# The gate in steps of four row groups, one wait for the row scatters of a half, a shorter warm-up and a new issue order

## The chip, the cores and the metric

The kernel runs on one core of a Trainium2 chip. The core has five engines that run their own instruction streams: TensorE (matmuls, PE in the profile, with its weight loads as PEld), VectorE (DVE), ScalarE (ACT), GpSimd (POOL) and SyncE (SP, which only issues transfers here). The metric is the time of one execution in microseconds on the device; the median over runs is compared.

## The reference, cut to what matters

A spectral layer is followed by a mixture of experts with two levels of routing.

```
X = rfft(x, axis=1)                                  # x: 8 x 1856 x 256
Y = soft_threshold(X @ (w_r + i w_i) + b, 0.01)      # real and imaginary part by themselves
x = irfft(Y).reshape(14848, 256)
...
g = argmax(x @ w_group); g_w = softmax at g           # 4 groups
e = argmax(x @ w_expert[g]); e_w = softmax at e       # 4 experts in the group
out[t] = g_w * e_w * (relu(x[t] @ w1[g, e]) @ w2[g, e])   # 256 -> 1024 -> 256
```

## The kernel before, in words

The 8 sequences are taken as 4 pairs. The first part of the program (up to about 476 us) works on the pairs one after the other, and overlaps the stages of one with those of its neighbours; the second part works through the experts.

Stages of a pair: the first transform's matmuls and VectorE's transposes of their results (`first_a`, L362, and `turn_a`, L403; for the last chunk of the first pair two half chunks, L411 and L414), 15 steps of the second transform and the weight matmuls (L697, L761) with splits into high and low parts on ScalarE and VectorE, then the inverse (`b_mm`, L809, `p_mm`, L828 and L831, with ScalarE's copies into the row tile in `p_out`, L839 and L841). The rows of a pair are in two halves of 16 row groups each. For eight units u of a pair, four to a half, TensorE turns the rows (`p_turn`, L850), ScalarE copies them to `yt` (L854), the gate's matmuls (`g_mm`, L871) form the logits of group and expert, and VectorE transposes these to `L` (`g_turn`, L881). Per half, `route_g` makes one-hot choices and slot numbers in 32 steps, mostly small VectorE instructions, and `scatter` (L305) writes the rows to a list for each expert in memory by GpSimd's indirect DMAs, 16 to a half, 128 in all. `FLY` says how many scatters are on their way at a time: two for the first three pairs, four for the last.

Eight early jobs of 256 rows (expert lists of the first 512 slots, 4 experts) are computed while the last pairs are routed: fetch of the rows by SyncE (`e_fetch`, L501 and L506; the first jobs wait for 64 scatters, the later ones for 96), transpose and split (L510, L936, L940), up matmuls (`up_mm`, L951), relu and split (L957, L961), down matmuls (`down_mm`, L972 and L973), scaling (L979, L984) and the store by GpSimd (`store`, L607). The second part, planned in `JOBS`, does the rest with the up matmuls in L549 and the down matmuls in L621 and L622.

In the first part the order of work is written out by hand: `ORDER` is a string with one letter for each step, and each letter calls the next step of its kind. On TensorE, ScalarE, VectorE and SyncE the instructions are issued in the order of the string. Letters used in this text: c and d the first transform and its transpose, o the end of a spectral step, v and w the inverse's last matmuls and copies, x and y the turn and its copy, G and H the gate's matmuls and their transpose, R a step of the routing, S one scatter, l a load on SyncE's queue, F an early job's fetch, W and V the split of an expert's weights, U and D the up and down matmuls of an early job (a quarter of each), K a store.

Ahead of all this, matmuls on constants warm TensorE up: 14 of 256 columns (L423) and 4 more (L427) ahead of the first data matmul, and 8 (L446) behind the second chunk.

Of the kernel before, what the change touches and what calls it, by code (L numbers as in the profile page):

```python
# [10 lines left out]
F32 = mybir.dt.float32  # L11
# [63 lines left out]


ORDER = """
efegjfhjihtugegiiktuekqpmqogpftmhmouccjkfeioqmhgotpjuimkmeqooftjphegudmiZmokcgqfhtoiujdpfktemqomhoupjmogimekfq
ocpghtjiukfdmqoehtmopgejiufmkmhqoetZgoupjgmkmidftqccioohudjpkmfmqehpcdgitmoofejmuhtoogkequgpjidmlkfitomcZqhopj
udmflkeoqpthmoujgimmfkqtoeZZhoujpemmfZkoogjqriphtfuesmsgokihrmoqjtpZfugsmskiZqmoehgrtoujpseimgskfrqihsmtosuepm  # L80
ofcdcdjkvvgiwhwoqtepmmcojZucdkfxqpmothuegoyxdjfimokqlyhvgcGwtdmocpjmilftukmHqhoeugpojximfketqygZhmpedocmfuojvg
himZwtdokeqpojugmkfxqyihmopmcdfvtuoGHjwRRvoRkqRepRhmwZiotjegRZRulikRRfxqmmtRhyoojpRugfegmRkZixqmptRZiRhyfomRoh
jvmuwGRokeRoqHgpjRxtmRmuRyRifRRtooleghkqirupjRsmRksofZtqhmoursjepmRkRmvqgRRfooihewjtRgsupxmmRReoikyfSoqtghrjsu
iGpfkSsHrRRqhetRmmpRgSoRSSsfmsohSuiSRjtcvkRmeRuqRpedgcowmcofmRljhRioSekdqdRtxypgRuoRvgfvjSwiSkxRwRyqitpchmvGRl
omufmdocRmjRhRtRkeHqdpwgReRucmiofgoScjhmRkdoRSiqoxSRyStRSpxjRuRfmmkqooReypRdcjmgthvduGRHfmioRRRtvRRwkegqwRpohi
mReSSRxuRfjkohRRmRegSiyRlSSqRtxRRuSpojSRkSvymfvRmwgShRoGRqSRwStpoHuxRjfmhiykemRqtSoRgSoRRRjSixypufRmhRmeoSokRq
tGHRSjRSrpRumkRseSsgimSqSfrRohptuSogeisRSjfRgsmRhkimqrSotRoRpsjeSufshmSmokgotjrWqpRumiWsfRRkqmResShopovRgRmRlt
oujmwSivkRoReqRRjfhptRSguxRkRfSRwimehmRqRSptWooRxuRRjmRykSqmRfygReitopSgohvvVfhiuSSSwGSjVxWSeSVkwRWmxygtVymHqp
WSGmviuHvoofjmkRRheoqRRRRwRRoRwRjtRSRpmRVugSRovfmvRRiekSwRVtgRRqSRwxhpojuSiRfekxRRhmmytRRoSlqogSRuRSRSpjyRmRfR
SixWWxGSkmhoHqytSouySSVRegjiVpmkmqoofGhtpujHRRRkmRqRRpSoRRRRSRmoSRmSmooFRTRRRXrRYSURRssFRSUSABrARRBRSsUsSRRRRR  # L90
RRrUsAARsSBBDIrWWDIlssVDvWVEwvTXDVSSwxYxWVSSUSyvyJvGWSHARBwESwxxSyUySWGHRRvRRvRRSRUwRwRxAWVRSRSBWSVVxAURyyRvRR
RlwSRvJGSSwxRxRRRRVHASRSFByKFBRyRRRDRDTXRYRRGHUAERSBURADSUBFUTASDXSRRJRDBAWYVEBKJSSWUWRRRUIDKTRlAWIESBRRDVRSRA
BRURURDSVVAXJRRDSRABERYRWBWDKFSWlJFRUUVKRVETDAWAWIRJWBUWVVBFVVAUSVBXRRYDRREASURSRBSDKUJlSRDRAWVWWKDABWUSBESVUV
DKASWTJDXBSASYBTSISSVUVDSESUAASJSSKSSRBKUEISDBUJADXYDABUBDKUIEAJBEKAUBDUAJBKADBEDDJDDKEJKEJK
"""

_OFF = {}
# [88 lines left out]
def spectral_moe(ctx: ExitStack, tc: tile.TileContext, x, wri, bri, wgate, w1, w2, cst, out):  # L186
    nc = tc.nc
# [108 lines left out]
        nc.vector.tensor_tensor(out=base, in0=base, in1=incf.rearrange("p (e r) -> p e r", e=NE)[:, :, n - 1], op=ALU.add)  # L296
        yield

    pend, sent, sent_of = [], [], []
    landed = mybir.DependencyInfo(mybir.DependencyClass.Sync, mybir.DependencyReason.DATA)  # L300

    def scatter(n):
        for _ in range(n):
            pr, sl_, row = pend.pop(0)
            ins = nc.gpsimd.indirect_dma_start(out=xs_d, out_offset=bass.IndirectOffsetOnAxis(ap=sl_, axis=0), in_=row,  # L305
                                               in_offset=None, bounds_check=ROWS - 1, oob_is_err=False)
            if len(sent) >= FLY[pr]:
# [29 lines left out]
    rt = inv.enter_context(tc.tile_pool(name="rt", bufs=1))  # L337
    ci = inv.enter_context(tc.tile_pool(name="ci", bufs=1))
    wi = inv.enter_context(tc.tile_pool(name="wi", bufs=2))
# [79 lines left out]
            pass  # L419

    warm = pg.tile([128, 512], F32, name="pg")
    for _ in range(14):
        nc.tensor.matmul(warm[:, 0:256], lhsT=ones, rhs=smask[16], start=True, stop=True)  # L423
    for _ in range(2):
        y = pw.tile([128, 512], F32, name="pw")
# [14 lines left out]
    for i in range(7):  # L440
        o = bank()
        first_a(0, i, o)
        turn_a(0, i, o)
        if i == 1:
            for _ in range(8):
                nc.tensor.matmul(warm[:, 0:256], lhsT=ones, rhs=smask[16], start=True, stop=True)  # L446
    for h in range(2):
        last_half(h)
# [199 lines left out]
    wts, raws, low, units, psum = {}, {}, {}, {}, {}  # L648
# [18 lines left out]
    pairs, later, u8, k15 = range(NP), range(1, NP), range(8), range(K1)  # L667
# [165 lines left out]
    yts = {}  # L833

    @steps_of(pairs, u8)
    def p_out(pr, u):
        o = psum.pop(("p", pr, u)).rearrange("p (h s b d x) -> p b x s h d", h=2, s=4, b=2, x=2)
        y = four(pr, u).rearrange("p b x (s h d) -> p b x s h d", s=4, h=2)
        nc.scalar.copy(out=y[:, 0], in_=o[:, 0])  # L839
        for h in range(2):  # L840
            nc.scalar.copy(out=y[:, 1, :, :, 1 - h], in_=o[:, 1, :, :, h])  # L841

    @steps_of(pairs, u8)
    def p_turn(pr, u):
# [5 lines left out]
                nc.tensor.transpose(o[:, c:c + 128], rows[:, i // 2, i % 2, ch * 128:ch * 128 + 128], ident)  # L850

    def p_copies(pr, u, copy):
        yts[pr, u] = wi.tile([128, 2, 4, 128], F32, name="yt", bufs=2)
        copy(out=yts[pr, u], in_=psum.pop(("t", pr, u)).rearrange("p (c r t) -> p c r t", c=2, r=4))  # L854

    copies = iter([(pr, u) for pr in pairs for u in u8])
# [3 lines left out]
            p_copies(*next(copies), copy)  # L860
            yield

    @steps_of(pairs, range(0, 8, 2))
    def g_mm(pr, u):
        psum["g", pr, u] = pg.tile([128, 512], F32, name="pg")
        o = psum["g", pr, u][:, 0:256].rearrange("p (h v z) -> p v h z", h=2, v=2)
        for v in range(2):
            yt = yts.pop((pr, u + v)).rearrange("p c (h x) t -> p c h x t", h=2)
            for ch in range(2):
                for q in range(4):  # L870
                    nc.tensor.matmul(o[32 * q:32 * q + 32, v], lhsT=wg[:, ch], rhs=yt[:, ch, :, :, 32 * q:32 * q + 32],  # L871
                                     start=ch == 0, stop=ch == 1)
# [574 lines left out]
```

## Time and profile before

| | us |
|---|---|
| three runs | 1066.43, 1066.68, 1061.5 (median 1066.43) |
| the profiled execution | 1063.61 |
| its span from the first to the last instruction | 1061.8 |
| TensorE busy | 1015.5 (96%) |
| VectorE busy | 698.5 (66%) |
| ScalarE busy | 545.9 (51%) |
| GpSimd busy | 259.1 (24%) |

The rows further down come from the profiled execution. Matmuls are pipelined and their ends are modelled, so a TensorE that counts as busy is not always at its peak. An engine's idle time matters where it is the one that others wait for. "issue" and "remote" as the reason of a wait say that the profile shows nothing that ended it.

### The profile page before, as it was taken

What the parts mean: (1) busy time and instruction counts of PE and PEld (TensorE: products, weight loads), DVE (VectorE), ACT (ScalarE), POOL (GpSimd) and SP (SyncE); (2) the same over time, 40 slices, a digit from 0 to 9 for tenths busy, and PEclk for the clock granted to TensorE, in tenths of its full rate; (3) what the DMA queues carried; (4) which work ended last, traced back from release to release, by engine and by line L of the source; (5) the groups of instructions that cost most, each with busy time, mean ns of one, the idle gap of its engine ahead of it and who ended that gap; (6) DMA issues with size and microseconds to landing.
All of it is one profiled execution on the core that took longest, in us unless ns stands there. A gap on an engine that the chain in (4) does not pass through costs nothing.

```text
span 1061.8 us, 20038 instructions
## 1 busy us (share of the span) xinstructions
PE 1015.5 (96%) x7094; PEld 863.6 (81%) x7094; DVE 698.5 (66%) x1744; ACT 545.9 (51%) x1428; POOL 259.1 (24%) x267
## 2 busy tenths in 40 slices
PE   8999999899898987899999999999999999999996
PEld 5886887587776676788889989999889899889995
DVE  5888789688789555546667656466465566566551
ACT  3765675575783642334554445355354455454541
POOL 2000003236354545441112111211111212112121
PEclk9999999999999998999999999999999999999998
DMA  9435552332134354446434241432341420732100
GB/s 375 183 142 199 202 221 88 112 119 77 42 109 116 108 135 131 154 121 195 135 113 111 69 133 33 140 112 55 119 141 38 141 81 26 193 115 58 37 26 26
DMA packets 110932, 125.63 MB, mean 118 GB/s; under 512 B 86869, under 2 KB 87643, under 8 KB 105965
## 3 DMA queue, kind: packets, MB, share of 16 engines
q1 hardware_dynamic: 91549, 74.28, 23.8%
q0 software_dynamic: 12448, 30.68, 7.8%
q10 hardware_dynamic: 6832, 19.36, 4.7%
q8 instruction: 57, 0.93, 0.4%
q14 instruction: 46, 0.38, 0.1%
HBM read 74.32 MB, written 51.65 MB: 119 GB/s over the span
## 4 chain that ended last, share of the span: by engine, by line
PE 85%; issue 4%; DVE 4%; POOL 1%; DMA 1%; ACT 1%; another core or an unknown queue 1%; SPq 0%; POOLq 0%; DVEq 0%; ACTq 0%
PE ph L549 25%; PE py L621 16%; PE pw L761 12%; PE py L622 8%; PE pg L697 5%; PE ph L951 4%; PE bank L809 3%; PE bank L362 2%; PE bank L850 2%; PE pg L972 2%; PE bank L828 2%; PE pg L871 1%; PE pg L973 1%; PE py L641 1%
## 5 line engine op out<-in xcount | busy, mean ns | idle before, releaser
L621 PE MATMUL py<-big,hh 128*128 128x512 f32 (+2 forms) x792 | 276.4, 393 | 0.3 <-DVE yo L629 0.3
L549 PE MATMUL ph<-xth,big 128*128 128x384 f32 (+17 forms) x1024 | 274.1, 345 | 1.1 <-DVE hl L557 0.7
L607 POOL DMA_INDIRECT out_dram<-yo,si x119 | 122.9, 1033 | 495.0 <-DVE si L327 239.2
L557 DVE SCALAR_TENSOR_TENSOR hl<-ph,hh 128x256 fp32r<-128x256 f32 x472 | 157.5, 372 | 97.7 <-ACT hh L553 70.8
L622 PE MATMUL py<-big,hl 128*128 128x256 f32 (+2 forms) x792 | 220.8, 279 | 0.0
L553 ACT ACTIVATE hh<-ph 128x256 fp32r<-128x256 f32 x472 | 140.0, 345 | 112.9 <-PE ph L549 109.9
L305 POOL DMA_INDIRECT xs_d<-v,sloti x128 | 127.4, 995 | 289.4 <-DVE xs L736 157.4
L549 PEld LDWEIGHTS ph<-xth,big 128*128 128x128 f32 x1024 | 185.6, 188 | 13.1 <-ACT xth L535 1.2
L549 PE MATMUL ph<-xtl,big 128*128 128x384 f32 (+17 forms) x512 | 176.5, 345 | 0.9 <-DVE xtl L536 0.6
L621 PEld LDWEIGHTS py<-big,hh 128*128 128x128 f32 (+2 forms) x792 | 147.1, 186 | 34.9 <-issue 0.8
L622 PEld LDWEIGHTS py<-big,hl 128*128 128x128 f32 (+2 forms) x792 | 147.5, 186 | 0.4
L629 DVE SCALAR_TENSOR_TENSOR yo<-py,si,yo 128x256 f32<-128x256 f32 (+3 forms) x99 | 47.8, 482 | 108.4 <-ACT yo L628 104.1
L628 ACT ACTIVATE yo<-py,si 128x256 f32<-128x256 f32 (+3 forms) x99 | 46.8, 473 | 130.7 <-PE py L622 109.1
L549 PEld LDWEIGHTS ph<-xtl,big 128*128 128x128 f32 x512 | 96.5, 188 | 6.1 <-DVE xtl L536 1.1
L761 PE MATMUL pw<-wh,xh 128*128 128x256 f32 x360 | 81.1, 307 | 6.1 <-issue 2.7
L783 ACT ACTIVATE th<-pw,sg 128x256 f32<-128x256 f32 x120 | 60.5, 525 | 38.3 <-PE pw L761 26.8
L761 PEld LDWEIGHTS pw<-wh,xh 128*128 128x128 f32 x360 | 54.4, 189 | 28.4 <-issue 7.0
L761 PE MATMUL pw<-wl,xh 128*128 128x256 f32 x360 | 71.6, 280 | 0.2 <-issue 0.2
L761 PE MATMUL pw<-wh,xl 128*128 128x256 f32 x360 | 71.5, 280 | 0.0
L697 PE MATMUL pg<-CF,big 128*128 128x128 f32 x480 | 64.5, 277 | 4.1 <-DVE xs L736 3.1
L697 PEld LDWEIGHTS pg<-CF,big 128*128 128x128 f32 x480 | 58.4, 191 | 11.6 <-issue 3.9
L951 PE MATMUL ph<-xth,big 128*128 128x256 f32 x256 | 54.0, 298 | 6.7 <-ACT xth L936 3.2
(197 smaller groups left out, 1563.5 us busy)
## 6 DMA issues: line engine op xcount, KB each, us to landing
xt<-in_w_dram SPq DMA_DIRECT2D x22, 1024.0 KB
xs_d<-zero ACTq DMA_DIRECT2D x16, 1170.0 KB
whole<-in_w_dram SPq DMA_DIRECT2D x16, 1024.0 KB
xt<-in_x_dram SPq DMA_DIRECT2D x8, 1024.0 KB
xg<-xs_d SPq DMA_DIRECT2D x48, 96.0 KB
v<-in_x_dram SPq DMA_DIRECT2D x4, 1024.0 KB
big<-in_x_dram SPq DMA_DIRECT2D x7, 512.0 KB
xg<-xs_d SPq DMA_DIRECT2D x24, 128.0 KB
```

Source lines behind the costliest of these rows:

```text
L305: ins = nc.gpsimd.indirect_dma_start(out=xs_d, out_offset=bass.IndirectOffsetOnAxis(ap=sl_, axis=0), in_=row, in_offset=None, bounds_check ...
L549: nc.tensor.matmul(o[:, :w], lhsT=a_[:, ch, fs], rhs=b_[:, ch, 0:w], start=k == 0, stop=k == 5)
L553: nc.scalar.activation(out=hh[:, f, :m], in_=ov, func=AF.Relu)
L557: nc.vector.scalar_tensor_tensor(out=hl[:, f, :m], in0=ov, scalar=0.0, in1=hh[:, f, :m].bitcast(F32), op0=ALU.max, op1=ALU.subtract)
L607: ins = nc.gpsimd.indirect_dma_start(out=out, out_offset=bass.IndirectOffsetOnAxis(ap=ids.si[0:m, t:t + 1], axis=0), in_=ysb, in_offset=No ...
L621: nc.tensor.matmul(o, lhsT=hh[:, f, ts], rhs=w2b[:, :, f, :], start=f == 0, stop=f == 7, skip_group_check=True)
L622: nc.tensor.matmul(o[:, 0:D], lhsT=hl[:, f, ts], rhs=w2h[:, f, :], start=False, stop=f == 7, skip_group_check=True)
L629: nc.vector.scalar_tensor_tensor(out=ysb, in0=o[:, 0:D], scalar=gate_w, in1=ysb, op0=ALU.mult, op1=ALU.add)
L697: nc.tensor.matmul(f_view(pr, k)[:, ch, :, bt], lhsT=zys[pr][:, k, bt, ch * 128:(ch + 1) * 128], rhs=T_v[:, k, :], start=True, stop=True)
L761: nc.tensor.matmul(y[:, half * D:(half + 1) * D], lhsT=a_[:, ch, t], rhs=w_[:, t, ch], start=False, stop=True, skip_group_check=True)
L783: nc.scalar.activation(out=units["t", pr, k][:, ri], in_=psum["m", pr, k][:, ri * D:(ri + 1) * D], func=AF.Relu, bias=nlam, scale=sg_col(0 ...
L951: nc.tensor.matmul(o[:, i * 256:(i + 1) * 256], lhsT=a_[:, ch, fs], rhs=b_[:, ch, :], start=k == 0, stop=k == 5)
```

## The change

The gate takes four units in one step where it took two: 64 matmul instructions of the profile fill a whole bank of 512 columns, and one transpose of 128x512 follows. There are 8 such steps instead of 16; `yt` has four buffers instead of two and `L` one instead of two. `p_out` notes the last of its copies for each unit, and the first scatter of each half gets a dependency on the last copy of that half, so that the later scatters of the half need no wait for the copies. The warm-up has 8 and 3 matmuls where it had 14 and 8. The order string is new from the first line to the last; it has eight G and eight H less and is otherwise made of the same letters.

```diff
-efegjfhjihtugegiiktuekqpmqogpftmhmouccjkfeioqmhgotpjuimkmeqooftjphegudmiZmokcgqfhtoiujdpfktemqomhoupjmogimekfq
...
+ejfegifhteguijtkhuqkpegmmqgfopoijhtmmucfoikeqotgjhpukeqfimhgpcZtomdfmouoicjkZethuZqmojdgpikmfqoepthmojeufgdkgi
...
-    pend, sent, sent_of = [], [], []
+    pend, sent, sent_of, written = [], [], [], {}
...
+            if len(sent) % 16 == 0:
+                tc.add_manual_dep(ins.ins, written[pr, len(sent) % 32 // 4 + 3], landed, reason="later rows of the half need no wait of their own")
...
-    for _ in range(14):
+    for _ in range(8):
         nc.tensor.matmul(warm[:, 0:256], lhsT=ones, rhs=smask[16], start=True, stop=True)
...
-            for _ in range(8):
+            for _ in range(3):
                 nc.tensor.matmul(warm[:, 0:256], lhsT=ones, rhs=smask[16], start=True, stop=True)
...
         for h in range(2):
-            nc.scalar.copy(out=y[:, 1, :, :, 1 - h], in_=o[:, 1, :, :, h])
+            ins = nc.scalar.copy(out=y[:, 1, :, :, 1 - h], in_=o[:, 1, :, :, h])
+        written[pr, u] = ins.ins.name
...
-        yts[pr, u] = wi.tile([128, 2, 4, 128], F32, name="yt", bufs=2)
+        yts[pr, u] = wi.tile([128, 2, 4, 128], F32, name="yt", bufs=4)
...
-    @steps_of(pairs, range(0, 8, 2))
+    @steps_of(pairs, range(0, 8, 4))
     def g_mm(pr, u):
         psum["g", pr, u] = pg.tile([128, 512], F32, name="pg")
-        o = psum["g", pr, u][:, 0:256].rearrange("p (h v z) -> p v h z", h=2, v=2)
-        for v in range(2):
+        o = psum["g", pr, u].rearrange("p (h v z) -> p v h z", h=2, v=4)
+        for v in range(4):
...
-    @steps_of(pairs, range(0, 8, 2))
+    @steps_of(pairs, range(0, 8, 4))
     def g_turn(pr, u):
-        if u % 4 == 0:
-            logits[pr, u // 4] = rt.tile([128, 16, 32], F32, name="L", bufs=2)
-        L = logits[pr, u // 4].rearrange("p (h i) m -> p h i m", h=2)[:, :, 2 * (u % 4):2 * (u % 4) + 4]
-        nc.vector.transpose(out=L, in_=psum.pop(("g", pr, u))[:, 0:256].rearrange("p (h i m) -> p h i m", h=2, i=4))
+        logits[pr, u // 4] = rt.tile([128, 16, 32], F32, name="L")
+        L = logits[pr, u // 4].rearrange("p (h i) m -> p h i m", h=2)
+        nc.vector.transpose(out=L, in_=psum.pop(("g", pr, u)).rearrange("p (h i m) -> p h i m", h=2, i=8))
```

## Rows read from the trace of the kernel before

**Rows 1.** Busy time by stretch; columns: stretch, length, engines, granted clock, DMA, GB/s.

```profile
0.00:20.00 20.00, 15.99 (x114) 7.36 (x114) 11.42 (x16) 5.27 (x9) 7.18 (x10) 1.00 0.93 360
20.00:155.00 135.00, 134.50 (x1197) 109.45 (x1198) 109.96 (x232) 89.89 (x214) 0.00 (x0) 1.00 0.54 207
155.00:330.00 175.00, 161.06 (x1532) 125.07 (x1534) 142.95 (x350) 111.43 (x261) 70.09 (x70) 0.99 0.28 95
330.00:386.00 56.00, 51.58 (x469) 36.00 (x461) 36.67 (x82) 27.90 (x55) 27.52 (x28) 0.97 0.30 93
386.00:476.00 90.00, 78.93 (x493) 70.43 (x494) 48.75 (x114) 31.66 (x62) 45.05 (x47) 0.92 0.47 142
476.00:1062.00 586.00, 573.43 (x3298) 515.29 (x3296) 348.73 (x954) 279.74 (x829) 109.30 (x113) 0.99 0.33 96
```

**Rows 2.** The same view for four short stretches; engines are PE, PEld, DVE, ACT, POOL.

```profile
265.00:276.00 11.00, 8.26 (x62) 6.05 (x58) 6.57 (x16) 4.21 (x10) 6.35 (x7) 0.84 0.22 77
374.00:382.00 8.00, 5.55 (x52) 4.46 (x42) 4.01 (x11) 3.29 (x7) 3.23 (x4) 0.79 0.38 98
402.00:423.00 21.00, 15.27 (x65) 11.78 (x64) 9.07 (x24) 5.79 (x13) 11.33 (x12) 0.76 0.48 143
441.00:450.00 9.00, 5.41 (x25) 4.67 (x24) 3.25 (x7) 1.11 (x2) 6.21 (x7) 0.81 0.28 97
```

**Rows 3.** VectorE's timeline: start, length, instruction, idle ahead of it and its reason.

```profile
379.54 0.45 DVE L881 STREAM_TRANSPOSE L<-pg 128x256 f32<-128x256 f32 x1 [3.92 <-remote]
```

**Rows 4.** The chain of waits: start, length, what.

```profile
374.61 2.27 DMA xs_d<-v,sloti
...
380.26 3.78 DMA xg<-xs_d
...
468.54 1.43 PE ph L951 x12
```

**Rows 5.** TensorE's timeline at an early job and at the first main job.

```profile
386.30 0.39 PE L951 MATMUL ph<-xtl,big 128*128 128x256 f32 x1 [0.34 <-DVE xtl L940]
...
476.80 0.34 PE L549 MATMUL ph<-xth,big 128*128 128x392 f32 x1
```

**Rows 6.** The timeline of TensorE and VectorE in the first 18 us.

```profile
1.52 3.15 PE L423 MATMUL pg<-smask,ones 128*128 128x256 bf16 x14 [1.52 <-DVE smask L213]
...
5.45 2.13 PE L362 MATMUL bank<-big,cA 64*64 64x512 f32 x16
...
7.51 1.05 PE L446 MATMUL pg<-smask,ones 128*128 128x256 bf16 x8
...
9.64 6.23 DVE L403 STREAM_TRANSPOSE big<-bank 128x1024 f32<-128x1024 f32 x5 [0.46 <-PE bank L362]
```

**Rows 7.** Groups of instructions before 476 us: busy, mean ns, idle ahead and reasons.

```profile
L871 PE MATMUL pg<-yt,wg 128*32 128x128 f32 x512 | 17.7, 276 | 0.9 <-DVE xl L730 0.6 <-issue 0.3
...
L881 DVE STREAM_TRANSPOSE L<-pg 128x256 f32<-128x256 f32 x16 | 7.1, 441 | 18.4 <-PE bank L828 8.2 <-PE pg L871 5.5 <-remote 3.9
...
L414 DVE STREAM_TRANSPOSE big<-bank 128x512 f32<-128x512 f32 x2 | 1.4, 695 | 0.2 <-PE bank L411 0.2
```

**Rows 8.** GpSimd: the scatters' timeline, and the extra wait instructions of L305 (last).

```profile
174.17 0.97 POOL L305 DMA_INDIRECT xs_d<-v,sloti  x1 [0.93 <-DMA xs_d<-v,sloti]
...
184.00 0.97 POOL L305 DMA_INDIRECT xs_d<-v,sloti  x1 [0.43 <-issue]
...
387.81 0.97 POOL L305 DMA_INDIRECT xs_d<-v,sloti  x1 [9.67 <-DVE base L296]
...
434.01 0.97 POOL L305 DMA_INDIRECT xs_d<-v,sloti  x1 [0.31 <-issue]
...
460.75 0.97 POOL L305 DMA_INDIRECT xs_d<-v,sloti  x1 [0.30 <-issue]
...
L305 POOLq EVENT_SEMAPHORE  x46: 17/17/24911, 145.5 to 456.2; - x46
```

**Rows 9.** SyncE's timeline at the first main job.

```profile
463.52 0.38 SPq L501 DMA_DIRECT2D xi<-xs_d  x1
```

More of the change, by code (lines that the diff above doesn't have):

```diff
@@ L77 @@
 ORDER = """
-efegjfhjihtugegiiktuekqpmqogpftmhmouccjkfeioqmhgotpjuimkmeqooftjphegudmiZmokcgqfhtoiujdpfktemqomhoupjmogimekfq
[L79 to L92, printed above, removed]
@@ L93 @@
-BRURURDSVVAXJRRDSRABERYRWBWDKFSWlJFRUUVKRVETDAWAWIRJWBUWVVBFVVAUSVBXRRYDRREASURSRBSDKUJlSRDRAWVWWKDABWUSBESVUV
-DKASWTJDXBSASYBTSISSVUVDSESUAASJSSKSSRBKUEISDBUJADXYDABUBDKUIEAJBEKAUBDUAJBKADBEDDJDDKEJKEJK
+ejfegifhteguijtkhuqkpegmmqgfopoijhtmmucfoikeqotgjhpukeqfimhgpcZtomdfmouoicjkZethuZqmojdgpikmfqoepthmojeufgdkgi
+hccmmqotojidpumkeoqfhpmtojufgkmdqomepciohtjmumogfokjqeitgphudmkfeZqpilghmtucifoohtcjdmmkqooepugjkidmqmftooejph
+ukgimfomqehptogjuimkemqoofjthupmmgoefkorhqjiptgufmsskieZZomqrogtjpheusZksmimfoogqrhZjituspkmqfepmsgothilorfhus
@@ new lines @@
+emsjgtekmucvqdiopwgfmcvZoZidjmowothkvvwujqpwfkmemgqopmtmohjxfyuoehxykqxitpoZjuekxqfgihypymlcdtummomfgojGvHoioc
+ktjRheqpudgmkRliqReofhgimotjupewRkZqfhtvmgRcRRmiRdpwcoocRumejkmdfoxoytqdRpmjhucovkdgRmfeoRRqihtujRwpmxRkRRgRoi
+eZqymofpgRthjixmemRyuooRkRfgqtrhpuRslsZjRRmkRZfrReoihqtspgmsouvfjewgkihmtxqyiRopmmuRrosfjGhkmotsqeHRgRuZRrpojs
+mRRklemSqgRsSRoRopfhvjimtRcuedmokwgqcvRiSpSidfcwSRRhomtjuRRvRkRoRfewmSqhgRpeoStijmukfxdRqgmthpSiSSRyfeumomgoij
+vhoRwSRRckqegdtpoxjxlumoyfRkxRqRphRilyRytmumSRfcRcotdGSdScSmvRhoRRRlojkuqSHRewjpgmidRmfRtRSkSeqpmRSRhSRSfovRgS
@@ new lines @@
+oomRcRhjeuowitkSjxygqpuRfdmmkeSqRRpvRovSiRRoStRgRmifjhuhRmkRqwSooteRpwugxjmSRfRkxyqoSmxRRitRpyheoRyujRRmRRgefR
+mhSSkqSSriRpGotgsiomfsutHorhessjRugikemrgRqopsSSSRjskmfmtqRohorpujRsseRmRkfWmRivvRSWSSwqtRpoSRRRWhogjRRxRuRmRR
+SSkfSihewRRSRoyvvRRmotgRqpuRjwikRRSRfRmRmeqwxgotVhpSioxyeSVmujWkxVyqfphoVtyGvSfhRHmSomlWRogjmSRvRuiRweRRRSkxRt
+WoSqRpjVwSugSRkRSRRqfimRSSoRSxtpSyyhemeSRfomSRRuvoRRggvhjkwRiRSRSmxwqRtRpiySWouRRjRxfRymRRhemogkSSoRGtuqHSjRil
+kRqSpRRmRfopRtmeRmhoumofgSSojithkuRSqRjkSRRpSRRqmpRmRRVmRRoSRmRRooSorRFTXRYSsFURsRrRRRSABsUIUAsSARrBRWDVSRSUss
@@ L95 @@
+ArVBBWWTSXDSsDSsSSWvvSYWwwDvRvSwVSEVVUAxwyESUxSlBASVJWUBJVxyWxyUSvySvGwAWVwvHSVASvRDBWwwSRRxIBFRVRFyTKlxRRDXRD
+lREYRyJDxRRRUURRFxRARBRRABRREUyRUTyARJRKKRXRGYRRAWBRBDRWTKUURRAABDUHVWIRSRIRBWUREXRDIRSJRRFDARSRVWVYRRVBABRlWE
+RRSVJRRSSSWDURSSKSVWVAWFVSUIWDDSASFSSlRDEKSVBJWUVBEJURWATRRRDRBARXBWVYRRRDRUWKURRSAASVSVSBIDUSVSBSWWEKJUDRSTVD
+SSAABXVBEYUSTDAEBJKSSUDAUBSSUDASXKEIBJDYABUJAUABKDDKBUAEUJDKADBEBDJDDKEJKEJK
 """
```

## The prediction

> **What bounds the kernel now.** I read the busy time of every engine by stretch first [rows 1]. From 476 us on TensorE is busy 573.4 of 586 us, at a clock of 0.99. Nothing in the diff is executed there, and 12.6 us of idle in 586 leave little to move. The same holds from 20 to 155 us: 134.5 of 135. TensorE is idle for 4.0 us before 20 us, 13.9 us from 155 to 330, 4.4 us from 330 to 386 and 11.1 us from 386 to 476: 33 us, and these are the places that another order can reach. VectorE is the runner-up from 20 to 330 us, with 253 of 310 us (82%), and drops to 54% after 386 us.
>
> Next I looked at where those idle stretches cost twice. Four windows [rows 2] hold a TensorE idle time and, right after it, a lower granted clock: 0.84, 0.79, 0.76 and 0.81 as means, which is some time at the half level (1.2 of 2.4 GHz). Each is priced as idle plus lost clock: 2.74 + 0.16 x 11 = 4.5 us; 2.45 + 0.21 x 8 = 4.1 us; 5.73 + 0.24 x 21 = 10.8 us; 3.59 + 0.19 x 9 = 5.3 us. Together 24.7 us of a 1061.8 us span. In all four several engines stand at once and the profile names mostly "issue" or "remote" as the cause, so I cannot say what ends them, only who stands where. In the second, VectorE stood 3.92 us at L881, the first of the two gate transposes of the last half, until 379.54 us [rows 3].
>
> Third, the chain of waits from 343 to 392 us [rows 4]: it runs through the row scatters on GpSimd's queue to the last scatter that the third early job needs (374.61), the fetch of its rows (380.26) and its first up matmuls. But TensorE itself waited only 0.34 us for that job [rows 5]; until then it had other steps to do. So the scatter queue is the longest chain there and still worth almost nothing on TensorE by itself.
>
> **The change part by part.**
>
> *Shorter warm-up.* Before the first data matmul 6 of 14 warm-up matmuls go, 3.15/14 = 0.225 us each, 1.35 us; behind the second chunk 5 of 8 go, 1.05/8 = 0.13 us each, 0.66 us [rows 6]. The first data matmul starts at 5.45 us, right behind the warm-up, so it is the warm-up that holds it and not its data. What counts is VectorE's transposes: five of them run without a gap from 9.64 us, and only the third had to wait, 0.46 us, behind the second warm-up block. Their data arrive meanwhile: 16 DMA engines are 0.93 busy in the first 20 us at 360 GB/s [rows 1], and the eight chunks of 524 KB and the weights' 524 KB need 4.7 MB / 360 GB/s = 13.1 us behind the first issue at 0.7, so the last half chunk cannot be much earlier than 14 us, where its matmul starts about 2 us later. Gain at most 1.35 + 0.46 = 1.8 us, at least nothing. I take 0.5, as the transfers and not the matmuls become what is late. On the other side, fewer warm-up matmuls may leave data matmuls at the half clock: the ratio is 0.225 to 0.13 for the same 256 columns, so the 2.13 us of the first two chunks would be 3.7 us, 1.6 us more, and with a third chunk some 2.4 us, of which 0.5 are regained: +1.9 us. That is the other bound.
>
> *The gate in steps of four row groups.* The 512 matmul instructions stay [rows 7]; a step is 64 instead of 32 (17.7/16 = 1.1 us, then 2.2 us). On VectorE 16 transposes of 128x256 (0.441 us each, 7.1 us) become 8 of 128x512; such a transpose from PSUM takes 0.695 us (L414), so 5.6 us: 1.5 us less. VectorE has 82% work before 330 us, so I count half of it, 0.7; bounds 0 and 1.5. In front of the 16 transposes VectorE stood idle for 18.4 us [rows 7], because it takes its instructions in order and the transpose comes before the gate's matmuls are done. Eight of those places vanish, and each of the others waits for 1.1 us more matmul and four copies instead of two. If all eight were exposed that is 8 x 1.1 = 8.8 us lost; if the waits halve, 9.2 us of VectorE idle is gained, most of it after 330 us, where VectorE has room. At nothing, then, but for the one place below. Four yt buffers for a step of four and two for a step of two give ScalarE the same wait (the copy after a full step waits for that step's matmuls); nothing, and one step of 2.2 us on ScalarE where the order leaves no cover. One L buffer instead of two: its reader and its writer are both VectorE instructions in order, nothing.
>
> *Scatters.* Each row scatter is 0.97 us on GpSimd. Where it needs a second wait, an extra wait instruction stands ahead of it (46 of them [rows 8]) and the idle before it is typically 0.93 us, without one 0.43 us. In the six halves with two scatters in flight, rows 2, 4, 6 and 14 have such a wait: 6 x 4 x 0.5 = 12 us of queue time go. The added dependency on the half's last copy sits on the first row, which waits anyway for its slot numbers, made from logits that come from those same copies: nothing. In the last two halves, with four in flight, the idle is 0.3 us with or without it. For TensorE the queue counted 0.34 us, so I take 0.3; bounds 0 and 4 us (the two halves ahead of the third early job).
>
> *The order.* Both strings hold the same letters but for eight G and eight H less. Counted by letters, ahead of the ninth U (the third early job's start) the new order has the same U, v, W and V, two D more and 18 R less: the last halves' routing moves behind it. Ahead of scatter 96 (first row of the seventh half) stand six U and four D more; ahead of scatter 112 one U and one D less. The loads l1 to l7 stand later in SyncE's queue, where nothing but loads stands at that time, and l13 to l15 earlier, l13 now ahead of the fetch of the fifth early job; the weight split that frees its buffer stands ahead of it in both strings, so the fetch is not held. No count shows less matmul work in front of any milestone, so the order can only win or lose idle time, up to 33 us plus the lost clock. The place where it plainly differs is the second stall: the VectorE instruction that stood there no longer exists, and the seventh and eighth halves' routing runs elsewhere. I take this one stall as gone, 4.1 us, and the others as staying. Bounds: none gone (0) and the two largest gone (10.8 + 5.3 = 16 us) on one side; the rival below on the other.
>
> **Sum.** The profiled execution took 1063.6 us (span 1061.8 and 1.8 around it), 0.3% under the median of 1066.43; the three runs shown lie between 1061.5 and 1066.7. 1063.6 - 0.5 - 0.7 - 0.3 - 4.1 = 1058.0 us.
>
> **A rule of the skill that speaks against the warm-up cut.** The Trainium skill, "TensorE: Matmul & The Clock Gate", section "Part 1: The HAM clock gate (the "warmup" mystery)", says that an array that has been idle begins at its lower clock and is raised only after sustained activity. The trace agrees so far: the first warm-up block runs at 0.225 us a matmul, the second at 0.13 [rows 6]. By that rule the cut would give the +1.9 us above in place of -0.5.
>
> **Rivals.**
>
> *Only the small terms arrive.* The stalls are not tied to the gate; they come back at other steps. For it: the first of the four lies in the spectral stage and the last two in early-job steps, none of which the gate touches, and nothing names their cause. Against it: VectorE's place in one of them is taken out. 1063.6 - 1.5 = 1062 us.
>
> *Two or more stalls go.* For it: the order is new from end to end. Against it: a new order meets its own hazards as well. 4.1 + 5.3 + 1.5: 1053 us.
>
> *The late halves end too late (slower).* The seventh half's scatters began at 387.81 us, the last half's at 434.01, the last one at 460.75; the first main job's rows are fetched at 463.52 [rows 8, 9] and its matmuls start at 476.80 [rows 5]. Six U and four D at 1.4 us each [rows 4] push the seventh half by 14 us to about 402; its 16 rows at 0.97 + 0.31 us and some five stores fill the queue to 429, so 5 us of cover are left, and the main job's rows have some 4 us more: for the third early job the way from the last scatter to the matmuls was 386.3 - 374.6 = 11.7 us [rows 4, 5], and 460.75 + 11.7 = 472.5. If the last scatter slips more than 9 us, TensorE waits. Slipping 15 us costs 6 us plus a half-clock stretch of 1.7 us: 1063.6 - 1.5 + 7.7 = 1070 us. For it: the whole of the routing of the last half stands behind more work. Against it: ahead of scatter 112 stand one U and one D less than before, and fewer stores stand between the last scatters.
>
> *The clock stays low at the start.* Everything else as forecast: 1058 + 2.4 = 1060 us.
>
> **How the numbers follow.** One stall gone 0.45 (own range 1054 to 1062), small terms only 0.20, two stalls gone 0.10, late halves 0.17, low clock 0.08. A difference under 0.5% (5.3 us, under 1061.1 or over 1071.8) is about what cannot be told from no change. Faster: 0.36 of the forecast's 0.45, the 0.10 and 0.02 of the low clock, 0.48. Slower: 0.12 of the late halves and 0.03 of the other cases, 0.15. The rest, 0.37, is no change. The range 1051 to 1067 leaves out the lower end of the two-stall case and most of the late halves, some 0.18.
>
> **What would show it.** Right: the first data matmul near 4.1 us at the full rate and the third transpose up to 0.5 us earlier; eight transposes at L881's place near 0.7 us with less idle than 18.4 us in sum; 20 to 24 extra waits fewer on GpSimd; no window like 374 to 382 us with a low clock; the first main matmul at about 471 instead of 476.8 us, and from there the same 585 us to the end. Wrong: the same number of half-clock stretches; a fetch for the first main job later than 463.5 us; or a main part that changes its own length, which I hold at nothing.

## The result, and the profile after

The kernel after takes 1077.66 us (median of four runs, 1073.92 to 1081.11) against 1064.59 of the kernel before (four runs, 1061.5 to 1066.68): a ratio of 1.0106, 95% interval 1.0068 to 1.0144. It is slower; the forecast was 1058.0 us, range 1051 to 1067. The profiled execution of after took 1081.11 us, with a span of 1079.2.

Busy time by stretch, kernel after, columns as in [rows 1] (length, PE, PEld, DVE, ACT, POOL, granted clock, DMA share, GB/s):

```profile
0.00:20.00 20.00, 14.39 (x103) 5.92 (x103) 11.43 (x16) 5.70 (x10) 7.15 (x10) 1.00 0.93 362
20.00:155.00 135.00, 134.29 (x1174) 109.50 (x1178) 109.70 (x231) 91.19 (x216) 0.00 (x0) 1.00 0.50 189
155.00:330.00 175.00, 157.94 (x1458) 123.04 (x1451) 130.80 (x312) 104.02 (x240) 65.96 (x67) 0.94 0.27 97
330.00:386.00 56.00, 50.10 (x399) 36.45 (x398) 36.99 (x77) 25.22 (x54) 28.11 (x29) 0.97 0.30 90
386.00:495.00 109.00, 92.70 (x662) 80.55 (x662) 59.63 (x148) 41.98 (x82) 49.96 (x51) 0.92 0.47 137
495.00:1080.00 585.00, 571.81 (x3294) 513.77 (x3292) 348.43 (x954) 279.50 (x829) 108.75 (x112) 0.99 0.33 96
```

The timelines of GpSimd, SyncE and TensorE around the end of the first part:

```profile
416.23 0.97 POOL L305 DMA_INDIRECT xs_d<-v,sloti  x1 [4.92 <-ACT hh L959]
...
476.72 0.97 POOL L305 DMA_INDIRECT xs_d<-v,sloti  x1 [0.30 <-issue]
...
479.48 0.38 SPq L503 DMA_DIRECT2D xi<-xs_d  x1
...
494.89 0.28 PE L975 MATMUL pg<-big,hl 128*128 128x256 f32 x1
495.01 0.34 PE L551 MATMUL ph<-xth,big 128*128 128x392 f32 x1
```

The first main matmul (L549 before, L551 after; most lines moved by two) starts at 495.01 us, not at 476.80 [rows 5]. From there to the end it is 584.2 us, before 585.0. So all of the loss, 18.2 us in the two traces, lies in the first part. Up to 155 us the two kernels run alike: 134.3 of 135 us, before 134.5. From 155 to 330 us TensorE idles for 17.1 us (before 13.9), and the granted clock is 0.94 (before 0.99) [rows 1].

Two counts of my own carry the rest; both are worked out from the records of the two traces. *Idle under the bursts*: a half's 16 scatters are a burst, from the start of the first to 3 us behind the start of the last. TensorE idles for 27.3 us under the eight bursts of the kernel before and 37.9 us under those of after, and for 2.1 and 1.3 us in all the rest from 165 to 490 us. *Half clock*: the clock is granted at its half level in 5 stretches of together 20.5 us before, in 9 of together 41.0 us after, the end of the program left out. The changes from 165 to 490 us are 10.6 - 0.8 = 9.8 us of idle under and outside the bursts, and 20.5/2 = 10.2 of lost clock: 20.0 us, somewhat over the 18.2, since part of the half-clock time is idle itself. The first 20 us hold 1.6 us more idle, but there 1.8 us of warm-up matmuls are gone. All four stall windows of [rows 2] lie in or just behind a burst as well. Bursts are frequent, though: in the kernel before they cover 232 of the 325 us from 165 to 490.

The scatters' waits, kernel after (the extra waits, then two reasons of idle time ahead of scatters, with their counts):

```profile
L305 POOLq EVENT_SEMAPHORE  x22: 17/17/15163, 154.2 to 472.7; - x22
...
  DMA xs_d<-v,sloti: 45.6, 51
  issue: 23.4, 69
```

24 of the 46 extra waits [rows 8] are gone. Of the 120 steps from one scatter of a half to the next, 87 are shorter than 1.5 us, before 77, and the bursts are 9 us shorter together.

### The profile page after: what moved, and what is told of

It reads as the page before. It is cut to its first block, busy times and chain, and to the rows that moved or that the text cites. A ratio compares the mean times of both kernels' runs of the same rounds, so it can differ in the third digit from the quotient of the medians.

```text
span 1079.2 us, 19960 instructions
## 1 busy us (share of the span) xinstructions
PE 1021.2 (95%) x7083; PEld 869.2 (81%) x7083; DVE 697.0 (65%) x1736; ACT 547.6 (51%) x1428; POOL 259.9 (24%) x267
## 4 chain that ended last, share of the span: by engine, by line
PE 83%; DVE 6%; issue 5%; ACT 2%; another core or an unknown queue 1%; DMA 1%; POOL 1%; SPq 0%; POOLq 0%; ACTq 0%; DVEq 0%
PE ph L551 25%; PE py L623 15%; PE pw L763 11%; PE py L624 8%; PE pg L699 5%; PE ph L953 3%; PE bank L811 3%; PE bank L853 3%; PE bank L830 2%; PE pg L974 2%; PE bank L364 2%; PE pg L874 1%; PE pg L975 1%; PE py L643 1%
## 5 line engine op out<-in xcount | busy, mean ns | idle before, releaser
L551 PE MATMUL ph<-xth,big 128*128 128x384 f32 (+17 forms) x1024 | 273.9, 345 | 1.1 <-DVE hl L559 0.7
L305 POOL DMA_INDIRECT xs_d<-v,sloti x128 | 128.3, 1002 | 301.6 <-DVE oh_g L234 166.7
L551 PEld LDWEIGHTS ph<-xth,big 128*128 128x128 f32 x1024 | 185.4, 188 | 13.0 <-ACT xth L537 1.3
L551 PE MATMUL ph<-xtl,big 128*128 128x384 f32 (+17 forms) x512 | 176.2, 344 | 0.9 <-DVE xtl L538 0.6
L551 PEld LDWEIGHTS ph<-xtl,big 128*128 128x128 f32 x512 | 96.4, 188 | 6.2 <-DVE xtl L538 1.1
L763 PE MATMUL pw<-wh,xh 128*128 128x256 f32 x360 | 83.6, 315 | 12.6 <-issue 6.7
L763 PEld LDWEIGHTS pw<-wh,xh 128*128 128x128 f32 x360 | 56.7, 197 | 36.7 <-issue 12.0
L763 PE MATMUL pw<-wh,xl 128*128 128x256 f32 x360 | 73.8, 288 | 0.0
L763 PEld LDWEIGHTS pw<-wh,xl 128*128 128x128 f32 x360 | 57.4, 196 | 0.2 <-issue 0.2
```

What stands on the lines that cost most here:

```text
L551: nc.tensor.matmul(o[:, :w], lhsT=a_[:, ch, fs], rhs=b_[:, ch, 0:w], start=k == 0, stop=k == 5)
L763: nc.tensor.matmul(y[:, half * D:(half + 1) * D], lhsT=a_[:, ch, t], rhs=w_[:, t, ch], start=False, stop=True, skip_group_check=True)
```

## What the traces show that no view names

TensorE's stalls end for "issue" or "remote", no reason. The trace also records when each semaphore is updated. I set each update of TensorE against the last modelled end of a matmul that makes such an update. From 20 to 155 us every update comes within 0.3 us. From 160 us, ahead of the first scatter, to the main part, 18 of 204 recorded updates come more than 1 us behind in the kernel before (up to 6.7 us) and 33 of 210 in the kernel after (the expectations below count from 165 to 495 us, and so 224 and 204 updates). All of them come within 5 us of the start of a scatter. None of VectorE's or ScalarE's that are recorded is that late in this part, and none of TensorE's in the main part before the end of the program, where GpSimd issues 104 further indirect DMAs, spread over 585 us. An instruction that waits for such an update stands with all its inputs ready, everything queued behind it stands too, and TensorE then pays with half clock. What is late may be the update or the matmul itself: the ends are modelled, so the trace can't tell.

Two more counts bear on this. All of the program's 7094 matmuls (7083 after) have their records, so the idle time is no gap in the records of matmuls. But update records are missing, of every engine and mostly under the bursts: in the kernel before 85 of VectorE's 326 there and 55 of ScalarE's 220, and none from 20 to 155 us or between the bursts. So it isn't shown that only TensorE is affected, nor whether the recording itself has a part in the stalls.

Theories: (1) the new order costs; (2) the longer gate steps cost; (3) the way in which the scatters follow each other, changed by the one wait, costs; (4), formed after the second set of runs: what costs is late updates of TensorE, brought about by dense scatters, on some chips only.

## The experiments

Six sets, each on one chip with its own runs of the kernel before. A is the chip of the first measurement. Columns: ratio to before with its interval; steps between scatters under 1.5 us; TensorE's idle time under the bursts; updates more than 1 us late; start of the first main matmul. All but the ratio come from one trace each; the kernel before has a trace on A alone. The record names five different chips for B to F and none for A, which could be one of them. Each was used in one set, so what differs between chips can't be told from what differs between sets.

| run | chip | ratio | short steps | idle, us | late | main at |
|---|---|---|---|---|---|---|
| before | A | 1 (1064.59 us) | 77 | 27.3 | 18 | 476.8 |
| after | A | 1.0106 [1.0068, 1.0144] | 87 | 37.9 | 33 | 495.0 |
| a_old_order | B (before 1076.41) | 1.0262 [1.0199, 1.0326] | 92 | 52.9 | 29 | 518.5 |
| b_warm_only | B | 0.9999 [0.9957, 1.0041] | 72 | 38.0 | 19 | 486.0 |
| c_wait_only | B | 1.0163 [1.0097, 1.0230] | 83 | 38.5 | 25 | 492.9 |
| d_gate_only | B | 0.9965 [0.9931, 1.0000] | 79 | 34.3 | 19 | 483.7 |
| u_gate_again | F (before 1064.98) | 1.0010 [0.9988, 1.0032] | 72 | 27.5 | 20 | 476.6 |
| y_fly4_third | F | 1.0562 [1.0528, 1.0596] | 102 | 58.6 | 34 | 537.7 |
| f_after_no_wait | C (before 1036.18) | 1.0016 [0.9998, 1.0034] | 75 | 6.0 | 0 | 447.9 |
| h_fly1 | C | 1.1048 [1.1017, 1.1078] | 21 | 107.8 | 0 | 553.3 |
| i_fly4 | C | 0.9911 [0.9886, 0.9936] | 100 | 3.3 | 0 | 435.3 |
| k_no_rows | C | 0.9902 [0.9874, 0.9930] | 74 | 3.5 | 0 | 441.7 |
| o_after_again | D (before 1036.02) | 1.0007 [0.9987, 1.0026] | 81 | 6.0 | 0 | 446.8 |
| s_wait_again | D | 0.9972 [0.9955, 0.9989] | 86 | 3.3 | 0 | 443.1 |
| p_after_fly4 | D | 0.9939 [0.9916, 0.9961] | 101 | 5.6 | 0 | 442.0 |
| q_fly4_again | D | 0.9882 [0.9854, 0.9911] | 102 | 3.3 | 0 | 435.3 |
| t_no_wait_again | E (before 1036.29) | 1.0030 [1.0009, 1.0050] | 69 | 6.0 | 0 | 450.8 |
| v_gate_fly4 | E | 0.9942 [0.9921, 0.9963] | 103 | 5.6 | 0 | 441.7 |
| w_no_rows_again | E | 0.9869 [0.9839, 0.9899] | 77 | 3.3 | 0 | 436.7 |
| x_wait_fly4 | E | 0.9897 [0.9872, 0.9923] | 100 | 3.3 | 0 | 438.1 |

### Set 1 (chip B): the parts one by one

**a_old_order.** The kernel after with the order of before, less the first G and the first H of each half.

```diff
-ejfegifhteguijtkhuqkpegmmqgfopoijhtmmucfoikeqotgjhpukeqfimhgpcZtomdfmouoicjkZethuZqmojdgpikmfqoepthmojeufgdkgi
...
+efegjfhjihtugegiiktuekqpmqogpftmhmouccjkfeioqmhgotpjuimkmeqooftjphegudmiZmokcgqfhtoiujdpfktemqomhoupjmogimekfq
...
```

> The changed kernel with the old order string, from which only the first G and the first H of each half are taken out; the gate in steps of four, the dependency of the first scatter and the short warm-up stay. If the new order is what costs (theory 1), this is at the time before or up to 3 us under it, 1060 to 1066 us, and the first main matmul starts at 473 to 478 us. If the longer gate step costs (theory 2), or the faster scatter queue (theory 3), it is as slow as the changed kernel, 1074 to 1080.

Measured 1.0262 on B, above the 1.0106 of the kernel after on A and above the time that any theory gave. The loss is there without the new order; theory 1 falls.

**b_warm_only.** The kernel before with the short warm-up.

```diff
-    for _ in range(14):
+    for _ in range(8):
...
-            for _ in range(8):
+            for _ in range(3):
```

> The kernel before with 8 and 3 warm-up matmuls. All theories: within 0.2% of before; by the prediction's term 0.5 us less. If the clock stayed low at the start, up to 2 us more and a lower granted clock in the first 20 us.

Measured 0.9999: nothing.

**c_wait_only.** The kernel before with the dependency of each half's first scatter, and nothing else.

```diff
+            if len(sent) % 16 == 0:
+                tc.add_manual_dep(ins.ins, written[pr, len(sent) % 32 // 4 + 3], landed, reason="later rows of the half need no wait of their own")
```

> The kernel before with the dependency of the first scatter alone. Theory 1: 0 to 1 us less, the scatters of the first six halves some 12 us faster in sum, 24 extra wait instructions fewer. Theory 3 (the scatters' new pace brings the stalls): 5 us or more above before, with more half-clock stretches.

Measured 1.0163 [1.0097, 1.0230]: on B this line by itself costs about what the whole change does on A. (The median of the three runs behind it, 1086.05 us, lies only 0.9% above the 1076.41 us of the kernel before, somewhat under the interval, so the size is uncertain.) VectorE's timeline inside the first burst:

```profile
183.63 0.42 DVE L747 TENSOR_TENSOR xl<-xs,xh 128x256 fp32r<-128x256 f32 x1
190.37 0.49 DVE L773 SCALAR_TENSOR_TENSOR pw<-pw,sg,bias 128x256 f32<-128x256 f32 x1 [6.31 <-remote]
```

L773 waits for six matmuls that by their records ended at 183.66. Updates of TensorE came at 188.89 and 190.34 us, with no matmul running, and L773 started 0.03 us behind the second. TensorE's next matmuls, which go on in the same bank, stood 6.37 us. The same instructions stand in the same order as in the kernel before, so the wait changed only when the scatters go out. This stall is an example of a late update and not the wait's own: b_warm_only, on the same chip and without the wait, stands at the same instruction (its L771), for 3.58 us.

```profile
187.13 0.49 DVE L771 SCALAR_TENSOR_TENSOR pw<-pw,sg,bias 128x256 f32<-128x256 f32 x1 [3.58 <-remote]
```

Nor do the traces of c_wait_only and b_warm_only differ much as a whole: 38.5 against 38.0 us of idle under the bursts, 34.0 against 30.7 us of half clock, 25 against 19 late updates. The cost of the wait is shown by the times; by which stalls it arises is not.

**d_gate_only.** The kernel before with the gate in steps of four and four `yt` buffers, the old order less the first G and H of each half.

```diff
-    @steps_of(pairs, range(0, 8, 2))
+    @steps_of(pairs, range(0, 8, 4))
```

> The kernel before with the gate in steps of four and nothing else, with the old order less the first G and H of each half. Theory 1: 0 to 2 us less than before, VectorE's idle ahead of the gate's transposes under 18 us. Theory 2 (the longer step holds TensorE and makes the logits late): 5 us or more above before.

Measured 0.9965 [0.9931, 1.0000]. Theory 2 falls here.

### Set 2 (chip C): the pace of the scatters

**f_after_no_wait.** The kernel after without the dependency (the lines of c_wait_only taken out).

> The kernel after, without the wait of each half's first scatter: gate of four row groups, the new order, the short warm-up. Theory 3 (how the scatters follow each other costs): the scatters start a half as in the kernel before and have its 46 or so waits again; TensorE's idle time under the eight bursts of scatters falls from 37.9 us (after) to 27 to 34, and the time is that of the kernel before or up to 0.8% less (the new order bought 1.6% where the wait was in, between the run with the old order and the kernel after). Theory 1 (the new order costs): about 1% slower than before still. Theory 2 (the longer gate steps cost) was worth nothing in the run that had them alone.

Measured 1.0016. But the kernel before takes 1036.18 us on this chip, and not one update of TensorE in the four traces is late by more than 0.14 us. The idle time of 6 us is below the 27 to 34 expected, for a reason that I had not foreseen: the chip.

**h_fly1** and **i_fly4.** The kernel before with one, and with four, scatters on their way in the first six halves.

```diff
-FLY = (2, 2, 2, 4)
+FLY = (1, 1, 1, 4)
...
-FLY = (2, 2, 2, 4)
+FLY = (4, 4, 4, 4)
```

> The kernel before, with one scatter on its way at a time in the first six halves, where there were two; the last two halves keep four. Theory 3: each scatter then waits for the landing of the one before it, some 2.2 to 2.5 us from start to start for 1.3 to 1.6; if what stalls TensorE is that scatters are in flight together, its idle time under the first six bursts (18 us of 174 in the kernel before) falls below 9 us, though the bursts are half as long again. Rival, a fixed cost of each scatter (some 0.2 us of TensorE for each of the 128): the idle time under the first six bursts stays at 18 to 27 us, spread over a longer time. Either way the early jobs' rows land up to 30 us later, so the total may be longer; what tells the two apart is the idle time under the bursts before that.

Measured 1.1048, and the idle time rose to 107.8 us, which neither reading had. The waits of h_fly1 between 228 and 275 us (who waits for whom, total, times, longest) show why:

```profile
DVE v L818 <- DMA xs_d<-v,sloti: 29.9, 1, 29.9
...
PE bank L809 <- DVE v L818: 28.0, 1, 28.0
```

The next pair's rows can't be written over until the scatters have read the old ones: plain work behind a slow queue. The run tells nothing of theory 3.

> The kernel before, with four scatters on their way at a time in all halves, where the first six had two. Theory 3: the queue issues one each 1.28 us without waits, TensorE's idle time under the first six bursts rises from 18 us to 25 to 35, and the kernel is 0.7 to 1.6% slower. Rival, a fixed cost of each scatter: the idle time stays at 18 to 24 us, and the time within 0.5% of the kernel before.

Measured 0.9911, faster, which neither reading had, with 3.3 us of idle under the bursts and no half-clock stretch before the end. Theory 3 (dense scatters cost) is wrong on this chip.

**k_no_rows.** The kernel before, with the bound on the row number at 0, so that (nearly) no row is written.

```diff
-                                               in_offset=None, bounds_check=ROWS - 1, oob_is_err=False)
+                                               in_offset=None, bounds_check=0, oob_is_err=False)
```

> The kernel before, with every scatter issued but its rows left out: the bound on the row number is 0, so that (nearly) no row of the token lists is written, and the experts get empty lists. What is read is the part up to 476 us. Theory 3 in its form 'rows in flight': the stalls of TensorE under the bursts (27 us of idle time in the kernel before) fall below 8 us, and the first main matmul comes 20 to 30 us earlier than 476.8. Rival, the issuing on GpSimd (the descriptors, not the rows) holds the other engines: the stalls stay at 20 us or more.

Measured 0.9902; main matmuls from 441.7 us. There were no late updates on this chip to remove, so the run can't tell rows from issuing.

### Set 3 (chip D): the same kernels where no update is late

**o_after_again**, **s_wait_again** (c_wait_only again), **p_after_fly4** (the kernel after, all of `FLY` at 4) and **q_fly4_again** (i_fly4 again).

> The kernel after, once more. In the traces of the kernel before, of the one after and of the first four runs, TensorE's semaphore updates come up to 10 us behind the modelled ends of its matmuls (18 of 224 by more than 1 us in the kernel before, 33 of 204 in the kernel after, all between 165 and 495 us, none of VectorE's or ScalarE's); in the second four runs, made on another chip, not one does, and the kernel before takes 1036 us there, not 1064 to 1076. Theory 4: what the change costs is more of these late updates. Where they occur, the ratio is 1.01 to 1.02 again, with idle time of TensorE under the bursts above that of the kernel before; on a chip where none is late by more than 0.3 us the ratio is 0.995 to 1.005. Rival (the wait of the first scatter costs by itself, through later halves): 1.008 or more on either chip.

> The kernel before with the one wait of each half's first scatter, as in c_wait_only, once more. Theory 4: where TensorE's updates come late, 1.01 to 1.02 again; where none does, 0.997 to 1.006, with the halves' bursts starting up to 5 us later than in the kernel before. Rival (the wait costs by itself): 1.01 or more on either chip.

> The kernel after with four scatters on their way in all halves. In the kernel before that took 0.9% off where no update came late, since the queue no longer waits for landings (12.8 us of idle time before scatters for a landing, 45.2 with two). Theory 4 with density as the cause of the late updates: where they occur, the time is 0.5 to 1.5% above that of the kernel after; where they don't occur, 0.5 to 1% below it. Rival (the waits for landings set the cost on any chip): 0.5% or more below the kernel after on either.

> The kernel before with four scatters on their way in all halves, as in i_fly4, once more. Theory 4 with density as the cause: 1.005 to 1.015 where updates come late, 0.99 where none does. Rival (waits for landings set the cost on any chip): 0.985 to 0.995 on either.

Measured 1.0007, 0.9972, 0.9939 and 0.9882, with no late update. The line that cost 0.9 to 1.6% on B gains 0.3% here, and the whole change is no change; all four fit theory 4, and "the wait costs by itself" falls. The two runs with four scatters fit their rival as well: both readings gave a gain here.

### Set 4 (chip E)

**w_no_rows_again** (k_no_rows), **t_no_wait_again** (f_after_no_wait), **x_wait_fly4** (c_wait_only with `FLY` at 4) and **v_gate_fly4** (d_gate_only with `FLY` at 4).

> The kernel before with every scatter issued but its rows left out (the bound on the row number is 0), once more. Where TensorE's updates come late in the other runs of this set: if the writing of the rows does it, none is late here, and the time is 3 to 4.5% below the kernel before; rival (issuing on GpSimd does it): late updates and some 25 us of TensorE idle under the bursts remain, and the time is within 1.5% of the kernel before. Where none is late: 0.990 again.

> The kernel after without the wait of each half's first scatter, as in f_after_no_wait, once more. Where updates come late: theory 4 with the wait as what makes the scatters collide more gives 0.990 to 1.002 (the kernel after: 1.0106 there); rival (the new order and the gate make them collide more) 1.008 to 1.015. Where none is late: 1.000 to 1.003 again.

> The kernel before with the wait of each half's first scatter and four scatters on their way in all halves. Where no update is late: the wait by itself gave 0.9972 and four on their way 0.988 to 0.991; if both come from the same idle time of the queue, 0.986 to 0.991 together; if they add, 0.984 to 0.988. Where updates come late: density as their cause gives 1.015 to 1.03; the waits for landings as their cause gives 0.98 to 0.995.

> The kernel before with the gate in steps of four row groups (the old order without the first gate steps of each half) and four scatters on their way in all halves. Where no update is late: 0.984 to 0.991, four on their way giving 0.988 to 0.991 and the gate steps 0 to 0.4% more (0.9965 by themselves, measured where updates come late). Where updates come late: density as their cause 1.00 to 1.015; the waits for landings as their cause 0.975 to 0.99.

Measured 0.9869, 1.0030, 0.9897 and 0.9942, again with no late update. With `FLY` at 4 the wait adds no gain, which fits that both take the same idle time out of the queue. The gate's steps look worse here than on B: 0.9942 with them, above the 0.984 to 0.991 expected, and 0.9882 to 0.9911 without (other chips). TensorE's last wait before the first main matmul shows where the rest goes, in o_after_again, t_no_wait_again and q_fly4_again, in this order:

```profile
446.82 0.44 PE L551 MATMUL ph<-xth,big 128*128 128x392 f32 x1 [3.84 <-ACT xth L537]
```

```profile
450.85 0.69 PE L549 MATMUL ph<-xth,big 128*128 128x392 f32 x1 [5.53 <-ACT xth L535]
```

```profile
435.26 0.44 PE L549 MATMUL ph<-xth,big 128*128 128x392 f32 x1 [0.58 <-ACT xth L535]
```

In the kernel after the last scatter goes out at 436.7 us on chip D, in q_fly4_again at 425.5; the main job's rows come too late for TensorE by 3.84 us.

### Set 5 (chip F): the decisive pair

**u_gate_again** (d_gate_only) and **y_fly4_third** (i_fly4).

> The kernel before with the gate in steps of four row groups alone (the old order without the first gate steps of each half), as in d_gate_only, once more. Where no update is late: theory 2 (the longer gate steps cost: half the logits come later, so the scatters and all that waits for them) 1.002 to 1.006, as the two runs with four on their way differ by 0.5%; rival (they save VectorE's time) 0.995 to 0.999. Where updates come late: 0.993 to 1.000 again.

> The kernel before with four scatters on their way in all halves, for the third time. Where updates come late: density as their cause gives 1.005 to 1.015; the waits for landings 0.985 to 0.995. Where none is late: 0.988 to 0.991 again.

Measured 1.0010 and 1.0562. Here updates come late again, so u_gate_again can't tell what the gate's steps cost where none is late. The kernel that was 0.9 to 1.2% faster on C and D is 5.6% slower; the direction is the one expected of density, the size is nearly four times the upper end of the 0.5 to 1.5% that I gave it. The idle time under the bursts doubles against u_gate_again, 58.6 for 27.5 us, with 34 late updates for 20. 31.1 us of idle and (88.7 - 20.5)/2 = 34.1 us of clock are 65 us; the main part starts 61.1 us later. The first stretch of the scatters' time, q_fly4_again (chip D) and then y_fly4_third (chip F), the same kernel:

```profile
165.00:330.00 165.00, 161.73 (x1561) 125.73 (x1563) 148.09 (x362) 110.52 (x257) 79.99 (x81) 1.00 0.31 102
```

```profile
165.00:330.00 165.00, 135.09 (x1119) 98.28 (x1115) 104.58 (x247) 80.25 (x189) 53.09 (x55) 0.87 0.19 66
```

And the same two in the first burst, all engines' timelines:

```profile
183.74 0.42 DVE L745 TENSOR_TENSOR xl<-xs,xh 128x256 fp32r<-128x256 f32 x1
...
184.07 0.48 DVE L771 SCALAR_TENSOR_TENSOR pw<-pw,sg,bias 128x256 f32<-128x256 f32 x1
...
184.48 0.97 POOL L305 DMA_INDIRECT xs_d<-v,sloti  x1 [0.30 <-issue]
184.62 0.50 PE L761 MATMUL pw<-wh,xh 128*128 128x256 f32 x2
```

```profile
182.35 0.59 ACT L709 CAST xh<-pg 128x512 fp32r<-128x512 f32 x1 [10.02 <-remote]
...
185.18 0.97 POOL L305 DMA_INDIRECT xs_d<-v,sloti  x1 [0.30 <-issue]
186.45 0.98 POOL L305 DMA_INDIRECT xs_d<-v,sloti  x1 [0.30 <-DMA xs_d<-v,sloti]
187.31 0.49 DVE L771 SCALAR_TENSOR_TENSOR pw<-pw,sg,bias 128x256 f32<-128x256 f32 x1 [8.28 <-remote]
...
187.85 0.79 PE L761 MATMUL pw<-wh,xh 128*128 128x256 f32 x2 [4.97 <-issue]
```

Compare the two lines of L771: on D it follows L745 at once, on F it stands 8.28 us for "remote" while GpSimd issues a scatter every 1.28 us undisturbed. On A, B and F the idle time under the bursts goes up with the number of short steps (72 to 79 steps: 27.3 to 38.0 us; 83 to 92: 37.9 to 52.9; 102: 58.6); on C, D and E it doesn't (100 to 103 steps: 3.3 to 5.6 us). That scatters in a denser row bring more late updates is shown by `FLY` on chip F, with the number on their way raised together with the density; that the one wait works through it is not shown, only read from the counts of single traces and from c_wait_only on B against s_wait_again on D.

The Trainium skill, "SBUF — State Buffer", section "Who interferes with whom", says that TensorE and ScalarE never wait on another engine's use of the memory, and that only VectorE and GpSimd contend. By that rule no scatter would hold TensorE at the memory. C, D and E agree (3.3 us of idle under q_fly4_again's bursts). On F it is 58.6 us, so something holds TensorE there; whether that is the memory, of which the rule speaks, isn't shown.

## Why the prediction was wrong, by its own steps

*The scatters: the step that failed.* The term was -0.3 us, with bounds of 0 and 4 us, both of them gains: queue time that goes, counted by what TensorE waited for the queue. The count itself was right (24 waits gone for 20 to 24 forecast, bursts 9 us shorter for 12). On D so was the bound: the wait by itself gains 0.28% of 1036, 2.9 us. On B, where updates come late, it costs 1.63% of 1076, 17.5 us (9.6 us by the medians). On A the step was not taken out of the kernel after: f_after_no_wait and t_no_wait_again ran on C and E, where the loss doesn't occur. So the wait's share of the 1.06% there is inferred from B. No loss side was priced for scatters that come closer together, though the unexplained stalls that I had priced at 24.7 us [rows 2] all lay under or right behind scatters, and the 135 us from 20 to 155, ahead of the first scatter, held 0.5 us of idle time [rows 1].

*The order, and one stall gone: -4.1 us.* I tied the stall at 374 to 382 us to the VectorE instruction that stood there [rows 3]. It started 0.02 us behind an update of TensorE that came 4.08 us after the matmul's modelled end, like the others. With that instruction gone the stalls came at others: half-clock stretches went from 5 to 9. "The order can only win or lose idle time" holds; whether the new one helps where the wait is in isn't shown (1.0106 on A against 1.0262 on B, two chips). Where nothing is late, order, gate and warm-up together make +0.16% (C) and +0.30% (E): no gain.

*The late halves* (rival, 0.17). The mechanism is real: the last scatter moved from 460.75 [rows 8] to 476.72 us and the fetch from 463.52 [rows 9] to 479.48. On A it decided nothing, as TensorE came out of its own stalls only at 494.9 and took the first main matmul at once. On D, with less delay ahead of it, the kernel after waits 3.84 us there.

*Warm-up: -0.5 us.* Nothing that the times show (0.9999 by itself). The timeline of the start, kernel after:

```profile
1.52 1.86 PE L425 MATMUL pg<-smask,ones 128*128 128x256 bf16 x8 [1.52 <-DVE smask L213]
...
4.73 2.22 PE L364 MATMUL bank<-big,cA 64*64 64x512 f32 x16 [0.48 <-DMA cA<-in_cst_dram]
...
6.88 0.50 PE L448 MATMUL pg<-smask,ones 128*128 128x256 bf16 x3
...
9.61 6.28 DVE L405 STREAM_TRANSPOSE big<-bank 128x1024 f32<-128x1024 f32 x5 [1.14 <-PE bank L364]
```

The data matmuls start at 4.73, not 4.1 us, as they now wait for the constants; the third transpose starts 0.03 us earlier [rows 6]. In this trace the low-clock rival isn't seen: the 16 matmuls take 2.22 us for 2.13. It is seen in the second trace of the same kernel, o_after_again:

```profile
4.90 3.69 PE L364 MATMUL bank<-big,cA 64*64 64x512 f32 x16 [0.66 <-DMA cA<-in_cst_dram]
```

3.69 us is the 3.7 of the prediction, and the last transpose of this part starts at 17.90 us for 16.66 before. It agrees with the Trainium skill's rule ("TensorE: Matmul & The Clock Gate", "Part 1: The HAM clock gate (the "warmup" mystery)"). The granted clock of the views can't tell here: it reads 1.00 in all of them, but o_after_again has no clock record ahead of 10.32 us, and the kernel after none ahead of 5.17. Of the seven traces with 8 matmuls ahead two show 3.69 us (the other is t_no_wait_again), the rest 2.22 to 3.14; with 14 ahead it is 1.95 to 2.93. So the rival does come in some executions, and costs there some 1.2 us for the +1.9 forecast; b_warm_only's interval of 0.4% to either side is too wide to show it.

*Gate: -0.7 us.* VectorE's work fell as forecast, 8 transposes of 0.710 us for 16 of 0.441 [rows 7], with the same idle ahead of them and not less (kernel after, group view before 495 us):

```profile
L883 DVE STREAM_TRANSPOSE L<-pg 128x512 f32<-128x512 f32 x8 | 5.7, 710 | 18.8 <-PE pg L874 13.0 <-remote 5.7
```

By itself the part is 0.9965 (B) and 1.0010 (F): between nothing and a third of a per cent.

*The main part* was held at no change, and is within 0.8 us.

Open: why A, B and F show late updates and C, D and E do not; whether the recording, whose update records are missing on the former (9913 to 10127 to a trace, for 12499 to 12580 on the latter), has a part; whether the matmul or its signal is late; and whether the rows' transfers or the issuing on GpSimd do it, since both runs without rows came to chips that show none. No version here is shown to beat the kernel before on every chip: four scatters on their way are 0.9 to 1.2% faster on C and D and 5.6% slower on F.

## What to carry to other kernels

When several engines stand at once and the profile names only "issue" or "remote", set the stalls against every other engine's bursts before the change is priced: here 27.3 of 29.4 us lay under GpSimd's scatters, which cover 71% of that time, and an edit that only "removes waits" from that queue cost 0.9 to 1.6% by itself on one chip. A wait that paces a queue can be worth more than the time it takes, so give such an edit a loss side. And a gain of 1% in one place is not a property of the kernel until a second chip has shown it.

## What I had not expected of the hardware

The same kernel takes 1036 us on three chips (C, D, E) and 1064 to 1076 us in the three other sets (A, B, F). TensorE's semaphore updates are up to 10.7 us behind the modelled ends of its matmuls in the latter (d_gate_only), only within 5 us of a scatter, and never by more than 0.14 us in that part on the former. Update records of all engines are missing under the bursts in the latter, and next to none on the former. With four scatters on their way the two kinds of chip are 1123.93 and 1023.54 us.
